# Queries in 576 columns instead of 640, and their positive part formed on GpSimd

## The chip, the cores and the metric

The kernel runs on one core of a Trainium2 chip. The metric is the device time of one execution in microseconds (us), given as the median of several runs. A profile of one execution stands beside it. Engines are called as the profile calls them: PE is TensorE, PEld its weight load, DVE is VectorE, ACT is ScalarE, POOL is GpSimd, and SP is SyncE, which here issues the transfers.

## The reference

An attention with a linear memory beside it is followed by two feed-forward products. B is 4, H is 8, S is 576, D is 64; the two products have 2048 and 1536 inner columns on a width of 512 and 2304 tokens.

```python
scores = q @ k^T / sqrt(D), causal;  a = softmax(scores);  local = a @ v
phi(x) = where(x > 0, x, exp(x) - 1) + 1            # = min(exp(x), 1) + max(x, 0)
mem_out = (phi(q) @ M_prev) / (phi(q) @ z_prev + 1e-6)
out = g * mem_out + (1 - g) * local                  # g = sigmoid(beta), one per head
x = out as [B*S, H*D];  h = x @ w_in
g2 = softplus(h);  x2 = g2 @ w_out
y = ((x2 @ w_a) * (x2 @ w_b)) @ w_2
```

## The kernel before

Sixteen attention units come first, one for each batch and pair of heads; a head lies in 64 of the 128 partitions. Each unit loads q and k turned (`qr`, `kr`), splits them into a rounded part and a rest (`qh`, `ql`, `kh`, `kl`), forms three products of these parts for the scores (L517), and takes mask, minimum and scale of the scores on DVE (L527, one instruction each for four blocks of each of two heads). ACT takes the exponentials (L531), PE turns them (L597, L614), ACT and DVE copy them out of the PSUM banks (L603, L605, L617), and PE multiplies them with v (L627, L647). The last 64 queries of two units go through L669 and L538 together.

The memory path of a unit is `prep_v` (L496 to L499: ACT forms exp(q) in `ph` and max(q, 0) in `pos`), `prep_v2` (L502: DVE forms `ph = min(ph, 1) + pos`), and `memory` (L545: PE multiplies `ph` with the memory in L555; DVE forms `nm` in L559 and L560 and `mo` in L561). `memory` of unit n uses PSUM banks 2 and 3, between the scores of unit n+1 and the turns of unit n. `pos` is one buffer, `ph` has two. Behind it the sums of the exponentials (`ss` on POOL, L582, and `rs` on DVE, L587) are turned (L570), copied (`rt`, L571), sent to a small DRAM tensor `rsd` and read back to all partitions as `rb` (L573, L576); `xx = po * rb` (L643, L655) ends the unit, and SP stores it (L660).

From the first units on, DVE and POOL also prepare the first feed-forward stage: L758, L759, L761 and L762 on DVE rebuild pieces of `w_in` from `raw`; L771 and L343 on POOL form their sums and rests; L801 reads finished tokens back from `xs` into `raw`. After the attention, PE runs the products of the first stage (L876) and later stages (L876, L1020) to the end.

The program is recorded as steps. `Plan.order` orders all steps of all engines once, at build time, in a simulated run with estimated durations; steps with the longest chain behind them go first, and PE takes attention before the first stage. Two rules in it concern POOL: DVE steps that read and write only SBUF are not placed while a POOL step runs, and a POOL step waits for the last such DVE step placed before it. Each engine then executes its own list in order.

In the kernel before, q has 640 columns. Columns 512 to 639 hold the last 64 queries of the two heads of a pair, each in 64 columns of its own with zeros in the other head's. L669 reads `u.qr[r, 512 + 64 * j : 576 + 64 * j]` and L555 reads column blocks of 64 from `ph`.

Of the kernel before, what the change touches and what calls it, by code (L numbers as in the profile page):

```python
# [12 lines left out]
AF = mybir.ActivationFunctionType  # L13
ALU = mybir.AluOpType
PSUM = bass.MemoryType.PSUM

B, H, S, D = 4, 8, 576, 64
NP = H // 2
# [305 lines left out]
def tile_kernel(ctx: ExitStack, tc: tile.TileContext, qt, kt, vt, mz, be, w_in, w_out, w_a, w_b, w_2, out):  # L324
    nc = tc.nc
    plan = Plan(tc)
    V, A, G, PE, SP = (
        Engine(plan, n, e) for n, e in (("DVE", nc.vector), ("ACT", nc.scalar), ("POOL", nc.gpsimd), ("PE", nc.tensor), ("SP", nc.sync))
    )

    def f(ap):
        return ap.bitcast(F32)

    def rnd(eng, o, i):
        if eng is A:
            A.activation(out=o, in_=i, func=AF.Copy)  # L336
        elif eng is V:
            V.tensor_copy(out=o, in_=i)
        else:
            G.tensor_scalar(out=o, in0=i, scalar1=1.0, scalar2=0.0, op0=ALU.mult, op1=ALU.add)  # L340

    def sub(eng, o, a, b):
        eng.tensor_tensor(out=o, in0=a, in1=b, op=ALU.subtract)  # L343
# [7 lines left out]
    bank = plan.track(nc.alloc_psum_tensor("bank", [128, 8, 512], F32).ap())  # L351
# [12 lines left out]
    def put(name, words, *at, dtype=F32):  # L364

        tag = name + "_" * (name in where)
        where[name] = [plan.buffer(f"{tag}{i}", words, a, dtype) for i, a in enumerate(at)], [0]

    def take(name):
        bufs, turn = where[name]  # L370
        turn[0] += 1
        return bufs[(turn[0] - 1) % len(bufs)]

    def space(lo):

        at = [lo]

        def next_(words):
            at[0] += (words + 7) & ~7
            return at[0] - ((words + 7) & ~7)  # L380

        next_.at = at
        return next_
# [12 lines left out]
    put("raw", 2048, RAW, RAW + 2048)  # L396
    early, late, spare = space(X1), space(X2), space(SUMS)
    more = space(WL + 7168)
    for n, words in (("kr", S), ("qr", 640), ("qh", 512), ("ql", 512), ("kh", S), ("kl", S), ("ph", 640)):
        at = [early(words), early(words)] + [more(words)] * (n in ("kr", "qr"))  # L400
        put(n, words, *at, dtype=F32R if n[1] in "hl" and n != "ph" else F32)
    put("pos", 640, early(640))
    w3 = [early(512) for _ in range(3)]
    put("eTrue", 512, *w3, spare(512), *(late(512) for _ in range(4)))
    put("eFalse", 256, *(spare(256) for _ in range(4)), *(late(256) for _ in range(4)))
# [26 lines left out]
    for j in range(2):  # L432
        G.affine_select(
            out=mask2[64 * j : 64 * j + 64, 1, 224:], in_=mask2[64 * j : 64 * j + 64, 1, 224:], compare_op=ALU.is_ge, fill=MASKED,
# [3 lines left out]
    both = (top, low)  # L438
# [24 lines left out]
    class Unit:  # L463
# [7 lines left out]
        def loads_k(self):  # L471
            b, p = self.b, self.p
            self.kr, self.qr = take("kr"), take("qr")
            first = b == p == 0
            for c, d in ((0, 256), (256, 640)) if first else ((0, 640),):
                SP.dma_start(out=self.kr[:, c : min(d, S)], in_=kt[b, p][:, c : min(d, S)])
                (A if first else SP).dma_start(out=self.qr[:, c:d], in_=qt[b, p][:, c:d])

        def loads_v(self):
# [5 lines left out]
        def prep_k(self, first=False):  # L485
            kr, qr = self.kr, self.qr
            self.qh, self.ql, self.kh, self.kl = (take(n) for n in ("qh", "ql", "kh", "kl"))
            e = V if first else G
            for c, d in ((0, 256), (256, 640)) if first else ((0, 640),):
                k, q = slice(c, min(d, S)), slice(c, min(d, 512))  # L490
                rnd(e, self.kh[:, k], kr[:, k])
                A.activation(out=self.qh[:, q], in_=qr[:, q], func=AF.Copy)
                sub(e, self.kl[:, k], kr[:, k], f(self.kh[:, k]))
                sub(e, self.ql[:, q], qr[:, q], f(self.qh[:, q]))

        def prep_v(self):  # L496
            self.ph, self.pos = take("ph"), take("pos")
            A.activation(out=self.ph, in_=self.qr, func=AF.Exp)
            A.activation(out=self.pos, in_=self.qr, func=AF.Relu)  # L499

        def prep_v2(self):
            V.scalar_tensor_tensor(out=self.ph, in0=self.ph, scalar=1.0, in1=self.pos, op0=ALU.min, op1=ALU.add)  # L502
# [42 lines left out]
        def memory(self, k):  # L545
            p, ph, mz = self.p, self.ph, mzs[self.b % 2]
            self.mo = mo = blocks(take("mo"))
            nm = take("nm")
            banks = bank[:, k : k + 2]
            s = banks[:, :, 0:325].rearrange("p j (c e) -> p j c e", c=5)  # L550
            for c in range(5):
                for half in both:
                    at = slice(128 * c + half.start, 128 * c + half.stop)
                    for j, r in self.rows:
                        PE.matmul(  # L555
                            out=s[half, j, c], lhsT=ph[r, at], rhs=mz[r, p], start=c == 0, stop=True, skip_group_check=True,
                        )
            by = lambda t: t.rearrange("p (j c) -> p j c", j=2)
            V.scalar_tensor_tensor(out=by(nm), in0=s[:, :, :, 64], scalar=1e-6, in1=by(self.rs), op0=ALU.add, op1=ALU.mult)  # L559
            V.reciprocal(out=nm, in_=nm)  # L560
            V.tensor_tensor(  # L561
                out=mo.rearrange("p c (j e) -> p j c e", j=2), in0=s[:, :, :, 0:64],
                in1=by(nm).unsqueeze(3).to_broadcast([128, 2, 5, 64]), op=ALU.mult,
            )
# [98 lines left out]
    def tails(at):  # L663

        for x in range(2):
            for u, k in at:
                for j, r in u.rows:
                    c = x ^ j
                    PE.matmul(  # L669
                        out=bank[both[j], k + c, :288], lhsT=u.qr[r, 512 + 64 * j : 576 + 64 * j], rhs=u.kr[r, 288 * c : 288 * c + 288],  # L670
                        start=True, stop=True, skip_group_check=True,
                    )
        for u, k in at:
            u.score_tail(k)
# [3 lines left out]
    def attention():  # L678
# [16 lines left out]
        for n in range(nu + 2):  # L695
# [24 lines left out]
            if cur:  # L720
                if n % 2 == 0:
                    nxt.begin()
                    tails(((cur, 0), (nxt, TAIL)))
                cur.sums()
                cur.over()
# [517 lines left out]
```

## Time and profile before

| what | value |
|---|---|
| median of 3 runs | 922.59 us (921.78 to 922.73) |
| profiled execution | 922.7 us, of which the profiled span is 920.9 us |
| granted TensorE clock | 1.0 over the whole span |
| busy PE, DVE, ACT, POOL | 907.3, 790.7, 565.3, 99.6 us |
| moved by DMA | 172.16 MB |

A share of busy time is a mean over very different stages. The attention ends near 176 us; POOL works only up to 169 us. Matmuls are pipelined, so PE counts as busy also where one matmul waits a little behind another.

### The profile page before, as it was taken

The numbers are of one execution on the slowest core, as the hardware profiler recorded it, in microseconds if no ns is written. First come the engines' busy times: TensorE is split into PE (matmuls) and PEld (weight loads), VectorE is DVE, ScalarE is ACT, GpSimd is POOL, SyncE is SP. The second block draws the span as 40 slices with busy tenths as digits, with TensorE's granted clock in tenths as the row PEclk, the third lists the DMA queues.
The fourth block names the chain that finished last, engine by engine and source line by source line (L and its number), as shares of the span: only waits on it lengthen the run. The fifth ranks groups of instructions, "written<-read, shape, count | busy, mean of one in ns | idle before, by whom it ended". The sixth has DMA issues, their size and how long they took to land.

```text
span 920.9 us, 17618 instructions
## 1 busy us (share of the span) xinstructions
PE 907.3 (99%) x6556; PEld 868.8 (94%) x6556; DVE 790.7 (86%) x1503; ACT 565.3 (61%) x1124; POOL 99.6 (11%) x140
## 2 busy tenths in 40 slices
PE   6999999999999999999999999999999999999998
PEld 4777777899999999999999999999999999999998
DVE  6999999889999758988599999988899666998683
ACT  7999999677666675744456655444444344555443
POOL 6445686100000000000000000000000000000000
PEclk9999999999999999999999999999999999999999
DMA  7656553368899889572620445455657156672701
GB/s 233 189 156 180 183 165 114 112 238 265 301 303 304 296 292 384 207 250 81 231 85 7 177 149 180 146 167 179 217 181 234 45 183 184 234 243 91 217 26 52
DMA packets 84838, 172.16 MB, mean 187 GB/s; under 512 B 8320, under 2 KB 60944, under 8 KB 82064
## 3 DMA queue, kind: packets, MB, share of 16 engines
q1 hardware_dynamic: 84320, 170.70, 56.4%
q8 instruction: 51, 0.84, 0.4%
q10 hardware_dynamic: 432, 0.33, 0.1%
q14 instruction: 35, 0.29, 0.1%
HBM read 110.90 MB, written 60.10 MB: 186 GB/s over the span
## 4 chain that ended last, share of the span: by engine, by line
PE 95%; DVE 2%; DMA 1%; issue 0%; SPq 0%; ACT 0%; DVEq 0%
PE bank L876 47%; PE bank L1020 33%; PE bank L627 4%; PE bank L597 3%; PE bank L517 3%; PE bank L555 1%; PE bank L669 1%; PE bank L647 1%; DVE eTrue L527 1%; PE bank L614 1%; DMA rb<-rsd 1%; PE bank L635 1%; DMA kr<-kt 0%; DVE ph L502 0%; DVE eT L538 0%
## 5 line engine op out<-in xcount | busy, mean ns | idle before, releaser
L346 DVE TENSOR_TENSOR s<-bank,s 128x384 f32<-128x384 f32 x216 | 118.0, 554 | 39.6 <-PE bank L876 30.5
L854 ACT ACTIVATE s<-bank 128x384 f32<-128x384 f32 x72 | 35.0, 486 | 80.7 <-PE bank L876 51.5
L343 DVE TENSOR_TENSOR t<-t,t 128x1536 f32<-128x1536 f32 (+1 forms) x48 | 74.6, 1554 | 0.4
L876 PE MATMUL bank<-x1h,w 128*128 128x384 f32 x240 | 70.7, 335 | 0.0
L876 PE MATMUL bank<-x5h,w 128*128 128x384 f32 x240 | 70.7, 335 | 0.0
L876 PE MATMUL bank<-x7h,w 128*128 128x384 f32 x240 | 70.6, 334 | 0.0
L876 PE MATMUL bank<-x3h,w 128*128 128x384 f32 x240 | 70.5, 334 | 0.0
L876 PE MATMUL bank<-x6h,w 128*128 128x384 f32 x240 | 70.5, 334 | 0.0
L876 PE MATMUL bank<-x4h,w 128*128 128x384 f32 x240 | 70.5, 334 | 0.0
L876 PE MATMUL bank<-x2h,w 128*128 128x384 f32 x240 | 70.5, 334 | 0.0
L336 ACT ACTIVATE w<-wf 128x256 fp32r<-128x256 f32 (+1 forms) x100 | 50.1, 501 | 19.6 <-DVE w L343 15.1
L912 ACT ACTIVATE s<-s 128x384 f32<-128x384 f32 x72 | 37.5, 523 | 33.2 <-DVE s L346 32.8
L851 ACT ACTIVATE s<-bank 128x384 f32<-128x384 f32 x72 | 34.9, 485 | 32.2 <-PE bank L876 14.9
L336 ACT ACTIVATE gx1h<-t 128x768 fp32r<-128x768 f32 x37 | 31.4, 848 | 34.0 <-PE bank L1020 33.5
L336 ACT ACTIVATE gx2h<-t 128x768 fp32r<-128x768 f32 x37 | 31.4, 847 | 34.0 <-PE bank L1020 32.9
L343 DVE TENSOR_TENSOR w<-wf,w 128x256 fp32r<-128x256 f32 (+1 forms) x90 | 47.5, 528 | 3.9 <-ACT w L336 3.5
L336 ACT ACTIVATE gx0h<-t 128x768 fp32r<-128x768 f32 x37 | 31.3, 846 | 30.6 <-PE bank L1020 29.1
L760 ACT ACTIVATE raw<-raw 128x512 f32<-128x512 f32 (+1 forms) x54 | 43.2, 801 | 9.8 <-DVE raw L759 9.2
L343 DVE TENSOR_TENSOR gx1l<-t,gx1h 128x768 fp32r<-128x768 f32 x37 | 35.4, 956 | 13.5 <-ACT gx1h L336 13.3
L343 DVE TENSOR_TENSOR gx0l<-t,gx0h 128x768 fp32r<-128x768 f32 x37 | 35.4, 957 | 13.0 <-ACT gx0h L336 12.8
L857 ACT ACTIVATE s<-bank 128x384 f32<-128x384 f32 x72 | 35.2, 489 | 16.2 <-PE bank L876 12.1
L336 ACT ACTIVATE gx3h<-t 128x768 fp32r<-128x768 f32 x36 | 30.4, 845 | 23.8 <-PE bank L1020 23.7
(340 smaller groups left out, 2992.1 us busy)
## 6 DMA issues: line engine op xcount, KB each, us to landing
gs<-s SPq DMA_DIRECT2D x96, 192.0 KB
t<-gs SPq DMA_DIRECT2D x24, 768.0 KB
us<-s SPq DMA_DIRECT2D x72, 192.0 KB
t<-us SPq DMA_DIRECT2D x12, 768.0 KB
raw<-w_out SPq DMA_DIRECT2D x8, 1024.0 KB
raw<-w_in SPq DMA_DIRECT2D x12, 512.0 KB
raw<-w_a SPq DMA_DIRECT2D x12, 512.0 KB
raw<-w_b SPq DMA_DIRECT2D x12, 512.0 KB
```

The lines of the kernel that those rows point to most:

```text
L336: A.activation(out=o, in_=i, func=AF.Copy)
L343: eng.tensor_tensor(out=o, in0=a, in1=b, op=ALU.subtract)
L346: eng.tensor_tensor(out=o, in0=a, in1=b, op=ALU.add)
L517: PE.matmul(out=s[:, j, at : at + L], lhsT=a[r, qc], rhs=b[r, 0:L], start=t == 0, stop=t == 2, skip_group_check=True,)
L627: PE.matmul(out=self.po[both[j], 128 * k :], lhsT=self.vr[:, k, 64 * j : 64 * j + 64], rhs=a, start=False, stop=k == 3, skip_group_check=True,
L760: A.activation(out=f(high), in_=f(high), func=AF.Identity, scale=REBIAS)
L851: A.activation(out=self.s1, in_=bank["b"], func=AF.Copy)
L854: A.activation(out=self.s5, in_=bank["c"], func=AF.Copy)
L857: A.activation(out=self.s2, in_=bank["b"], func=AF.Copy)
L876: PE.matmul(out=o, lhsT=w(n, a, k), rhs=x[n][c][:, k], start=start and k == t == 0, stop=k == 1 and t == 2, skip_group_check=True,)
L912: A.activation(out=s, in_=s if bank is None else bank, func=AF.Softplus)
L1020: PE.matmul(out=o, lhsT=self.w[n][a][:, u, 128 * m : 128 * m + 128], rhs=x[c][:, j], start=start and u == t == 0, stop=u == self.nu - 1 an ...
```

## The change

q is laid out in 576 columns: both heads' last 64 queries stand in columns 512 to 575, each in its own 64 partitions. The buffers of q, `ph` and `pos` shrink from 640 to 576 words, so the exponential on ACT and L502 on DVE work on 576 columns. max(q, 0) is formed by POOL instead of ACT. L555 reads columns 512 to 575 for both halves of the last block. The host no longer fills zeros.

```diff
-    for n, words in (("kr", S), ("qr", 640), ..., ("kl", S), ("ph", 640)):
+    for n, words in (("kr", S), ("qr", S), ..., ("kl", S), ("ph", S)):
...
-    put("pos", 640, early(640))
+    put("pos", S, early(S))
...
         def prep_v(self):
             self.ph, self.pos = take("ph"), take("pos")
             A.activation(out=self.ph, in_=self.qr, func=AF.Exp)
-            A.activation(out=self.pos, in_=self.qr, func=AF.Relu)
+            G.tensor_scalar(out=self.pos, in0=self.qr, scalar1=0.0, scalar2=0.0, op0=ALU.max, op1=ALU.add)
...
-                    at = slice(128 * c + half.start, 128 * c + half.stop)
+                    at = slice(128 * c + half.start, 128 * c + half.stop) if c < 4 else slice(512, S)
...
-                        out=bank[both[j], k + c, :288], lhsT=u.qr[r, 512 + 64 * j : 576 + 64 * j], rhs=u.kr[r, 288 * c : 288 * c + 288],
+                        out=bank[both[j], k + c, :288], lhsT=u.qr[r, 512:S], rhs=u.kr[r, 288 * c : 288 * c + 288],
...
-    qt = np.zeros((B, NP, 128, 640), q.dtype)
...
+        "qt": arr(split(q).transpose(0, 1, 2, 4, 3).reshape(B, NP, 128, S)),
```

Since the durations of steps change, `Plan.order` gives other lists for DVE, ACT, POOL and SP. PE's list stays, but for one place at the end of the attention, where four matmuls of L876 move from ahead of L615 of unit 15 to behind its L653.

The first place is DVE's list at the start of the program, where unit 0 (`ph0_78`, `nm0_129`, `mo0_103`) and the scores of unit 1 (`eTrue4_85` to `eFalse5_94`) meet. Before:

```order
L443 RECIPROCAL gt0_59<-gt0_59 128x8
L502 SCALAR_TENSOR_TENSOR ph0_78<-ph0_78,pos0_80 128x640
L538 ISA eT0_97,mn0_127<-bank,mask20_57 128x576
...
L527 ISA eFalse4_93,mn1_128<-bank,mask10_56 128x128
...
L559 SCALAR_TENSOR_TENSOR nm0_129<-bank,rs0_133 128x10
L527 ISA eTrue7_88,mn1_128<-bank,mask10_56 128x512
...
L560 RECIPROCAL nm0_129<-nm0_129 128x10
L571 COPY rt0_107<-bank 9x128
L561 TENSOR_TENSOR mo0_103<-bank,nm0_129 128x2x5x64
L527 ISA eFalse7_96,mn1_128<-bank,mask10_56 128x256
```

And of the change, at the same place:

```order
L443 RECIPROCAL gt0_59<-gt0_59 128x8
L538 ISA eT0_97,mn0_127<-bank,mask20_57 128x576
...
L527 ISA eTrue7_88,mn1_128<-bank,mask10_56 128x512
...
L527 ISA eFalse7_96,mn1_128<-bank,mask10_56 128x256
...
L527 ISA eFalse5_94,mn1_128<-bank,mask10_56 128x128
...
L502 SCALAR_TENSOR_TENSOR ph0_78<-ph0_78,pos0_80 128x576
L559 SCALAR_TENSOR_TENSOR nm0_129<-bank,rs0_133 128x10
L560 RECIPROCAL nm0_129<-nm0_129 128x10
L571 COPY rt0_107<-bank 9x128
L561 TENSOR_TENSOR mo0_103<-bank,nm0_129 128x2x5x64
```

L502 of unit 0 moved from ahead of the first L538 to behind all scores of unit 1, and `nm`, `rt` and `mo` moved behind it.

The second place is PE's list there, which is the same in both programs; L555 reads `ph0_78`, L570 turns the sums, L597 turns the exponentials:

```order
L517 MATMUL bank<-kh1_75,ql1_73 128x512 x2
L555 MATMUL bank<-mz0_105,ph0_78 64x65 x20
L570 MATMUL bank<-ident0_55,rs0_133 10x128
L597 MATMUL bank<-ident0_55,eFalse0_89 128x128
L597 MATMUL bank<-ident0_55,eFalse2_91 128x128
```

Nothing moved here: L555 of unit 0 stands ahead of all turns of unit 0, and of everything that follows.

The third place is SP's list around units 10 and 11, where `rb0_121` and `rb1_122` bring back the sums of both. Before:

```order
L660 DMA xs1<-xx1_124 128x384
L660 DMA xs2<-xx1_124 128x192
L483 DMA vr0_100<-vt 64x128
L801 DMA raw1_63<-xs0 128x1536
L573 DMA rsd11<-rt1_108 9x128
L576 DMA rb0_121<-rsd10 64x576 x2
L576 DMA rb1_122<-rsd11 64x576 x2
```

And of the change:

```order
L573 DMA rsd10<-rt0_107 9x128
L660 DMA xs1<-xx1_124 128x384
L660 DMA xs2<-xx1_124 128x192
L573 DMA rsd11<-rt1_108 9x128
L576 DMA rb0_121<-rsd10 64x576 x2
L576 DMA rb1_122<-rsd11 64x576 x2
```

L801, a read of 768 KB, no longer stands just ahead of these small transfers; it comes 20 transfers later, after the units 12 and 13 were sent.

## Rows read from the trace of the kernel before

**Rows 1.** The page's fourth part: the chain that ended last, shares by engine.

```profile
PE 95%; DVE 2%; DMA 1%; issue 0%; SPq 0%; ACT 0%; DVEq 0%
```

**Rows 2.** Windows: length; busy of PE, PEld, DVE, ACT, POOL; clock, DMA, GB/s.

```profile
24.40:44.80 20.40, 20.36 (x286) 15.72 (x286) 20.24 (x67) 19.91 (x54) 8.97 (x12) 1.00 0.61 189
44.80:65.20 20.40, 20.25 (x284) 15.72 (x284) 20.24 (x67) 18.48 (x52) 9.00 (x13) 1.00 0.52 159
65.20:85.50 20.30, 20.15 (x284) 15.71 (x284) 20.11 (x67) 18.95 (x54) 10.92 (x16) 1.00 0.50 151
85.50:105.50 20.00, 19.98 (x282) 15.53 (x282) 19.79 (x66) 19.94 (x57) 10.07 (x14) 1.00 0.68 199
105.50:125.20 19.70, 19.70 (x285) 15.39 (x284) 18.89 (x64) 18.70 (x53) 16.20 (x19) 1.00 0.56 174
125.20:146.10 20.90, 19.99 (x290) 15.49 (x288) 18.85 (x63) 20.47 (x58) 17.35 (x19) 1.00 0.47 138
...
176.00:921.00 745.00, 741.58 (x4276) 740.83 (x4275) 627.48 (x981) 404.63 (x687) 0.00 (x0) 1.00 0.57 191
```

**Rows 3.** Timeline of DVE, 10 to 27 us: start, duration, instruction, idle before it.

```profile
11.11 0.77 DVE L502 SCALAR_TENSOR_TENSOR ph<-ph,pos 128x640 f32<-128x640 f32 x1
12.35 0.76 DVE L538 CUSTOM_DVE_ANT_0 eT<-bank,mask 128x576 f32<-128x576 f32 x1 [0.47 <-PE bank L669]
...
16.79 0.21 DVE L560 RECIPROCAL nm<-nm 128x10 f32<-128x10 f32 x1
...
17.06 0.80 DVE L561 TENSOR_TENSOR mo<-bank,nm 128x640 f32<-128x640 f32 x1
17.79 0.40 DVE L527 CUSTOM_DVE_ANT_0 eFalse<-bank,mask 128x256 f32<-128x256 f32 x1
...
18.34 1.46 DVE L605 TENSOR_SCALAR aT<-bank,og 128x512 f32<-128x512 f32 x2
```

**Rows 4.** Timeline of PE, 14 to 25 us.

```profile
14.75 0.86 PE L555 MATMUL bank<-mz,ph 64*64 64x65 f32 x40
16.24 0.28 PE L570 MATMUL bank<-ident,rs 128*10 128x128 f32 x1 [0.63 <-DVE mn L527]
...
17.91 0.33 PE L597 MATMUL bank<-ident,eFalse 128*128 128x128 f32 x1 [0.27 <-DVE mo L561]
...
20.99 0.28 PE L570 MATMUL bank<-ident,rs 128*10 128x128 f32 x1 [0.56 <-DVE rs L587]
...
23.25 0.50 PE L517 MATMUL bank<-kh,qh 64*128 64x512 f32 x2 [0.57 <-ACT aT L603]
...
24.38 0.81 PE L555 MATMUL bank<-mz,ph 64*64 64x65 f32 x40 [0.17 <-DVE ph L502]
```

**Rows 5.** Groups by line and shape, DVE, 24.4 to 105.5 us: busy, mean ns, idle.

```profile
L527 DVE CUSTOM_DVE_ANT_0 eTrue<-bank,mask 128x512 f32<-128x512 f32 x16 | 10.7, 682 | 0.0
L527 DVE CUSTOM_DVE_ANT_0 eTrue<-bank,mask 128x384 f32<-128x384 f32 x16 | 8.2, 545 | 0.0
L502 DVE SCALAR_TENSOR_TENSOR ph<-ph,pos 128x640 f32<-128x640 f32 x9 | 7.4, 826 | 0.0
...
L759 DVE SCALAR_TENSOR_TENSOR raw<-raw 128x512 uint32<-128x512 uint32 x4 | 2.7, 670 | 0.0
...
L761 DVE TENSOR_SCALAR raw<-raw 128x512 f32<-128x512 f32 x4 | 1.6, 411 | 0.0
```

**Rows 6.** Groups by line and shape, all engines, 20 to 165 us.

```profile
L499 ACT ACTIVATE pos<-qr 128x640 f32<-128x640 f32 x15 | 11.0, 735 | 3.0 <-DVE ph L502 2.9
...
L340 POOL TENSOR_SCALAR kh<-kr 128x576 fp32r<-128x576 f32 x12 | 8.2, 680 | 6.9 <-PE bank L517 5.7 <-DMA kr<-kt 1.1
```

**Rows 7.** The chain in order of time, one piece: start, length, what.

```profile
124.55 5.73 DMA rb<-rsd
```

**Rows 8.** Timeline of all engines, 26.3 to 29 us.

```profile
26.47 1.41 POOL L343 TENSOR_TENSOR kl<-kr,kh 128x576 fp32r<-128x576 f32 x1
...
27.64 0.93 DVE L502 SCALAR_TENSOR_TENSOR ph<-ph,pos 128x640 f32<-128x640 f32 x1
```

More of the change, by code (lines that the diff above doesn't have):

```diff
@@ L398, in tile_kernel @@
     more = space(WL + 7168)
-    for n, words in (("kr", S), ("qr", 640), ("qh", 512), ("ql", 512), ("kh", S), ("kl", S), ("ph", 640)):
+    for n, words in (("kr", S), ("qr", S), ("qh", 512), ("ql", 512), ("kh", S), ("kl", S), ("ph", S)):
         at = [early(words), early(words)] + [more(words)] * (n in ("kr", "qr"))
         put(n, words, *at, dtype=F32R if n[1] in "hl" and n != "ph" else F32)
-    put("pos", 640, early(640))
+    put("pos", S, early(S))
     w3 = [early(512) for _ in range(3)]
@@ L474, in loads_k @@
             first = b == p == 0
-            for c, d in ((0, 256), (256, 640)) if first else ((0, 640),):
-                SP.dma_start(out=self.kr[:, c : min(d, S)], in_=kt[b, p][:, c : min(d, S)])
+            for c, d in ((0, 256), (256, S)) if first else ((0, S),):
+                SP.dma_start(out=self.kr[:, c:d], in_=kt[b, p][:, c:d])
                 (A if first else SP).dma_start(out=self.qr[:, c:d], in_=qt[b, p][:, c:d])
@@ L488, in prep_k @@
             e = V if first else G
-            for c, d in ((0, 256), (256, 640)) if first else ((0, 640),):
-                k, q = slice(c, min(d, S)), slice(c, min(d, 512))
+            for c, d in ((0, 256), (256, S)) if first else ((0, S),):
+                k, q = slice(c, d), slice(c, min(d, 512))
                 rnd(e, self.kh[:, k], kr[:, k])
@@ L1195 @@
     swap = lambda w: arr(w.reshape(-1, 128, 2, 2, 256)[:, :, :, ::-1]).reshape(w.shape)
-    qt = np.zeros((B, NP, 128, 640), q.dtype)
-    turned = split(q).transpose(0, 1, 2, 4, 3)
-    qt[..., 0:512] = turned[..., 0:512].reshape(B, NP, 128, 512)
-    for p in range(NP):
-        for j in range(2):
-            h = 64 * (j ^ (p & 1))
-            qt[:, p, 64 * j : 64 * j + 64, 512 + h : 576 + h] = turned[:, p, j, :, 512:576]
     def by_unit(a, axis):
@@ L1211 @@
     arrays = {
-        "qt": qt,
+        "qt": arr(split(q).transpose(0, 1, 2, 4, 3).reshape(B, NP, 128, S)),
         "kt": arr(split(k).transpose(0, 1, 2, 4, 3).reshape(B, NP, 128, S)),
```

## The prediction

> **What bounds the kernel now.** I read the chain first: 95% of the span hangs on PE and 2% on DVE [rows 1]. From 176 us to the end PE is busy 741.6 of 745.0 us [rows 2], and PE's list there is unchanged. So nothing behind 176 us can be won, and the question is only when PE gets there. Before 176 us I read the windows, cut where L555 of every second unit starts, so that each holds two units. The same PE list takes 20.4, 20.4, 20.3, 20.0, 19.7 and 20.9 us [rows 2]. The fastest, 19.7 us, has PE busy for all of it and DVE with 0.8 us to spare; I take it as what PE needs for two units. In the first three DVE is busy 20.24, 20.24 and 20.11 us, all but 0.2 us: there DVE sets the pace, and PE loses 0.7, 0.7 and 0.6 us, then 0.3. The sixth loses 1.2 us; a piece of the chain there is a read of `rb` that took 5.73 us [rows 7], queued behind L801, a read of 768 KB. All these losses are 3.5 us. Ahead of 24.4 us PE waits in larger pieces [rows 4]. These two places are all that the change can touch.
>
> **Part by part.** *Work taken from ACT and DVE.* ACT loses 16 of L499, 0.735 us each by its record [rows 6], and 64 columns of 16 exponentials. ACT has 0.1 to 1.9 us free in every window and is not what PE waits for, so I price this at nothing; the cover is DVE's own work, and were ACT the pace, 1.5 us per two units would come back. For DVE a 64-column piece costs half of 0.682 - 0.545 us, 0.07 us [rows 5]. Records overlap the next instruction a little (`mo`: 0.80 us by record, 0.73 us to the next start [rows 3]), so L502 occupies 0.75 us now and 0.68 us after; L759 0.60 us; L761 0.34 us.
>
> *The start.* L502 of unit 0 ran at 11.11 us in front of a DVE wait of 0.47 us that it cost nothing to fill [rows 3]. Now it stands behind unit 1's scores, while L555, which reads its result, still stands ahead of all PE work of unit 0. In DVE's list `nm`, `rt` and `mo` go behind it. There L560, L571 and L561 took 16.79 to 17.79 us, 1.00 us; without them the scores end at 18.34 - 1.00 = 17.34 us. Add 0.68 for L502 and 0.1 us to the start on PE (L597 started 0.05 us after `mo` ended): L555 starts at 18.1 instead of 14.75 us. It takes 0.81 us, so L570 follows at 18.9 instead of 16.24 us [rows 3, 4]: PE is 2.7 us late. It wins back waits that stood on that way: 0.27 for `mo`, 0.56 for `rs`, 0.57 for ACT, 0.17 us for L502 of unit 1 [rows 4], which now runs earlier in the list and is no longer late. That leaves 1.15 us at 24.38 us; small waits below these may take 0.15 more. I take +1.0 us. Bounds: 0 if the score instructions, freed of `nm` and `mo`, run ahead of PE by more than I think, and 2.7 us if none of the waits is won back.
>
> *The stretch from 24.4 to 105.5 us, with DVE as the pace.* From the lists: in the first window DVE has one L502 more and one L759 less; in the second one L502 less (and L762 becomes L759); in the third one L762 more, one L758 and one L759 less; in the fourth one L502 and two L761 less, one L758 more. L762 and L758 are close to L759 and L761. With 0.07 us less in each L502 DVE needs 20.24 + 0.68 - 0.14 - 0.60 = 20.2; 20.24 - 0.75 - 0.14 = 19.4; 20.11 - 0.14 + 0.60 - 0.34 - 0.60 = 19.6; 19.79 - 0.75 - 0.07 + 0.34 - 0.68 = 18.6 us. Where that is under 19.7 us PE is the pace. The sum is 20.2 + 3 x 19.7 = 79.3 us, against 81.1 now: -1.8 us. In the third window L502 stands right ahead of the scores of a new unit, which L555 waits for; I give back 0.3 us: -1.5 us. Bounds: -2.3 us (PE alone, 4 x 19.7) and 0.
>
> *105.5 to 176 us.* The fifth window has room for one L502 more. In the sixth L801 is gone from ahead of `rb`, but the rebuilding of the last `w_in` pieces has come here: L759 and two L761 more. DVE needs 18.85 + 0.60 + 0.68 - 0.14 = 20.0 us, against 20.9 now: -0.9 us. The last two L762 run near 150 us, 1.2 us more against one L502 less, 0.75 us, in a stretch with little room: +0.3 us. Together -0.6 us, bounds -1.4 and +0.5 us.
>
> *POOL.* Its new instruction is not in the trace. The nearest is L340, of the same size and with one input: 0.68 us [rows 6]; the far bound is the two-input L343, 1.41 us [rows 8]. I take 0.68 us, 10.9 us for 16. POOL is busy 39 of 81.1 us between 24.4 and 105.5 us [rows 2], so it has room. But its work for the first units of the next stage (sums and rests of `w_in` and x) gets later: by the lists 22 instructions of it follow the last new one. POOL was busy 16.2 and 17.4 us in the two windows in which it did much of this work, against 9 to 11 us before [rows 2], so some 13 us of it move back behind 150 us, where POOL was idle for more than half of the time; it ends perhaps 8 us later than at 169 us, near 177. PE takes these parts one after the other during its first two units of the stage, behind 176 us. I count them as just in time, with some 2 us of cover. If that cover is gone, PE waits for what is missing, one for one.
>
> *One rule against the change.* When L502 met a POOL instruction with two inputs, it took 0.93 instead of 0.81 us: POOL had run from 26.47 to 27.88 us, and L502 started at 27.64 [rows 5, 8]. The Trainium skill, SBUF — State Buffer, section "SBUF: two separate sides", says that a DVE operation with two SBUF inputs and a POOL operation that reads SBUF lock the shared port pair against each other, and that the loser waits for the whole of the other. By that rule L502 would have done nothing before 27.88 us and lasted 0.24 us longer; the row shows 0.12. The sum by the rule would add 10.9 us of locked time against DVE's L502, L759 and L762; by the row it adds a tenth of a microsecond for each meeting. I take the row.
>
> *The rest.* The read of q shrinks by 32 of 320 KB per unit; no wait of PE or DVE in [rows 3, 4] is for it: nothing. The moved four matmuls of L876 give PE 0.7 us less to do before L615, but DVE ahead of it has no L343 any more: nothing.
>
> **Sum.** 922.7 us of the profiled execution + 1.0 - 1.5 - 0.6 = 921.6 us. That execution is 0.1 us above the median of the runs, so I forecast **921.5 us** against 922.59.
>
> **Rivals.** *PE is the pace throughout.* All losses after 24.4 us go, 3.5 us, and the start costs 0.6: 919.7 us. For it speaks that DVE loses 80.4 - 77.8 = 2.6 us of work up to 105.5 us; against it, the first window, where hardly any of it goes.
>
> *The start costs all, little comes back.* +2.0 us at the start, -1.5 for the rest: 923.1 us. For it speaks the order of PE's list, which makes every matmul wait for `ph0_78`; against it, the 1.57 us of waits that lie behind it.
>
> *POOL and DVE block each other: slower.* Place: DVE's L502, L759 and L762, 24 instructions with two inputs from SBUF, between 24 and 165 us. POOL's share between 24.4 and 105.5 us rises from 48% to (39 + 8 x 0.68) / 81.1 = 55%, so 13 of them meet POOL if nothing keeps them apart. At 0.1 us a meeting it is nothing beside DVE's room. At half of an L343, 0.7 us, it is 9 us. From 0.25 us a meeting, 3.2 us in all on the path, the kernel is slower: 924.7 us. That the other eight L502 of [rows 5] took 0.81 us in the mean, (9 x 0.826 - 0.93) / 8, speaks against it: POOL's waits kept them apart; for it, that POOL has less time left to wait. The skill's section above is the rule that would bring this about.
>
> *The change does nothing at the end.* If start and stretch cancel, it is 922.6 us; this is inside my forecast's own range.
>
> **Chances and range.** My forecast, from -2.2 to 0 us, 44%; PE as the pace 28%; a dear start 13%; blocking 15%. A difference under 0.2%, 1.8 us, can hardly be told from none with this kernel. Faster by more (under 920.75): all of the PE case and a small part of mine, 34%. Slower by more: 14%. The rest, 52%, is the same. The range 919.3 to 924.0 us leaves out part of the PE case and most of blocking. The likeliest case alone spans 920.4 to 922.6.
>
> **What would show it.** Right: L555 of unit 0 starts near 18 us, and of unit 1 near 25.4 instead of 24.38; the next windows take 20.2, 19.7 to 20.0, and 19.7 us; no `rb` wait of DVE near 130 us; POOL ends near 177 us and PE has no gap from 170 to 190 us. Wrong: L502 of unit 0 starts at another time than 17.3; L502 records of 1 us and more with POOL beside them; DVE idle in a window that still takes over 20 us, which would name ACT or POOL as the pace; PE gaps after 176 us that wait for w or x rests from POOL.

## The result: slower by 0.7%, and the profile after

The changed kernel takes 929.81 us (median of 4 runs, 929.14 to 930.3) where the kernel before took 922.66 us beside it: 1.007 times as long, 95% interval 1.0058 to 1.0082. The forecast was 921.5 us with 924.0 us as its upper end. The profiled execution took 929.68 us, with a span of 927.9 us.

The chain that ended last, by engine, was 95% PE and 2% DVE [rows 1]. After the change:

```profile
PE 87%; DVE 5%; POOL 3%; issue 2%; DMA 1%; ACT 0%; SPq 0%; DVEq 0%; POOLq 0%; ACTq 0%
```

POOL, which had no share in it, now has 3%. What it has to do is in the groups by line and shape, 20 to 165 us, which answer to [rows 6]:

```profile
L499 POOL TENSOR_SCALAR pos<-qr 128x576 f32<-128x576 f32 x15 | 32.0, 2135 | 5.3 <-DVE ph L502 3.7 <-DMA rb<-rsd 1.0
...
L340 POOL TENSOR_SCALAR kh<-kr 128x576 fp32r<-128x576 f32 x13 | 8.9, 682 | 2.0 <-PE bank L517 1.7
```

The two lines have the same engine, kind of instruction and size, and one takes 2.135 us, the other 0.682 us. They also differ in the type that they write, float32 against fp32r; the run with the short L499 below writes float32 too and settles that.

Windows, cut as in [rows 2] (length; busy of PE, PEld, DVE, ACT, POOL; clock, DMA, GB/s), with one more from 97 to 132 us:

```profile
24.40:44.80 20.40, 20.13 (x282) 15.30 (x281) 19.96 (x66) 16.49 (x49) 14.46 (x15) 1.00 0.54 164
44.80:65.20 20.40, 19.87 (x284) 15.27 (x283) 20.00 (x67) 17.47 (x50) 13.65 (x14) 1.00 0.50 153
65.20:85.50 20.30, 20.30 (x291) 16.04 (x290) 19.92 (x66) 16.99 (x50) 12.87 (x14) 1.00 0.47 152
85.50:105.50 20.00, 19.40 (x280) 14.91 (x279) 19.35 (x64) 17.78 (x53) 16.44 (x18) 1.00 0.65 191
105.50:125.20 19.70, 18.98 (x278) 14.53 (x277) 17.64 (x58) 18.19 (x54) 17.04 (x19) 1.00 0.47 141
125.20:146.10 20.90, 18.98 (x257) 13.87 (x257) 19.30 (x65) 15.40 (x45) 13.77 (x13) 1.00 0.38 114
...
97.00:132.00 35.00, 32.49 (x449) 25.19 (x447) 30.88 (x99) 28.83 (x84) 29.58 (x30) 1.00 0.43 136
```

The last window in the kernel before:

```profile
97.00:132.00 35.00, 34.18 (x483) 26.08 (x479) 33.04 (x111) 33.88 (x96) 27.32 (x30) 1.00 0.50 156
```

Up to 125.2 us DVE has a little more idle time than before, as forecast, but PE loses 0.7 and 1.9 us in the two windows from 105.5 us on (0 and 0.9 before), and neither DVE nor ACT fills them. In the 35 us from 97 us PE is idle for 2.5 us, against 0.8 before.

The starts of L555 on PE, one mark per unit, show where the time goes (us from the start of the span; the last three columns are of experiments below):

| unit | before | changed | short L499 | unit 0 on ACT | q + 1 |
|---|---|---|---|---|---|
| 0 | 14.75 | 19.16 | 18.93 | 15.73 | 16.88 |
| 1 | 24.38 | 27.55 | 26.16 | 24.96 | 25.59 |
| 8 | 95.87 | 99.61 | 97.31 | 97.10 | 97.06 |
| 9 | 105.52 | 109.91 | 106.73 | 108.22 | 106.75 |
| 10 | 115.88 | 120.27 | 117.09 | 119.68 | 117.10 |
| 11 | 125.22 | 132.27 | 126.75 | 130.74 | 127.11 |
| 15 | 163.88 | 170.51 | 165.08 | 169.53 | 165.12 |

The changed kernel is 3.2 us late at unit 1, 3.7 at unit 8, 7.1 at unit 11, 6.6 at unit 15: two losses, one at the start and one between units 8 and 11. The first on PE's and DVE's timelines (answering to [rows 4] and [rows 3]):

```profile
19.16 1.36 PE L555 MATMUL bank<-mz,ph 64*64 64x65 f32 x40 [3.30 <-issue]
```

```profile
12.11 0.76 DVE L538 CUSTOM_DVE_ANT_0 eT<-bank,mask 128x576 f32<-128x576 f32 x1 [1.16 <-PE bank L669]
...
15.89 0.69 DVE L527 CUSTOM_DVE_ANT_0 eTrue<-bank,mask 128x512 f32<-128x512 f32 x1 [1.38 <-PE bank L517]
...
18.30 0.76 DVE L502 SCALAR_TENSOR_TENSOR ph<-ph,pos 128x576 f32<-128x576 f32 x1
```

L502 of unit 0 stands where the list put it, behind unit 1's scores, and PE stands still for 3.3 us until it is done. The page puts that wait down to "issue"; that it is for L502 is read from the list and from L502's end at 19.06 us.

The second loss on the chain in order of time (start, length, what), 122 to 131 us:

```profile
120.86 1.28 POOL w L343
122.15 0.66 POOL kh L340
122.80 0.07 issue
122.88 1.42 POOL kl L343
124.29 0.66 issue
...
125.00 2.13 POOL pos L499
...
127.21 0.22 POOL ss L582
...
127.45 0.04 DVE rs L587
...
127.58 0.69 DVE aT L605
128.27 1.10 DVE ph L502
129.38 0.66 DVE aT L605
130.04 0.60 DVE aT L617
```

From 120.86 to 127.43 us the links are work of POOL, one instruction behind the other, L499 the longest; the sums `ss` stand behind it, and DVE's `rs` waits for them. The 0.66 us at 124.29 us, which the chain calls "issue", is L499's wait for L502, which has still to read the one buffer of `pos`; L502 itself ran until `kl` had ended:

```profile
122.88 1.42 POOL L343 TENSOR_TENSOR kl<-kr,kh 128x576 fp32r<-128x576 f32 x1
123.27 1.64 DVE L502 SCALAR_TENSOR_TENSOR ph<-ph,pos 128x576 f32<-128x576 f32 x1
125.00 2.13 POOL L499 TENSOR_SCALAR pos<-qr 128x576 f32<-128x576 f32 x1 [0.70 <-DVE ph L502]
```

In the run called "q + 1" below, this stretch of the chain, 118 to 131 us, holds PE and 0.04 us of "issue".

### The profile page after: what moved, and what is told of

Read it like the earlier page. It is cut to its first block, busy times and chain, and to the rows that moved or that the text cites. A ratio compares the mean times of both kernels' runs of the same rounds, so it can differ in the third digit from the quotient of the medians.

```text
span 927.9 us, 17660 instructions
## 1 busy us (share of the span) xinstructions
PE 910.1 (98%) x6556; PEld 871.0 (94%) x6556; DVE 792.4 (85%) x1503; ACT 555.9 (60%) x1108; POOL 134.3 (14%) x156
## 4 chain that ended last, share of the span: by engine, by line
PE 87%; DVE 5%; POOL 3%; issue 2%; DMA 1%; ACT 0%; SPq 0%; DVEq 0%; POOLq 0%; ACTq 0%
PE bank L876 47%; PE bank L1020 33%; PE bank L627 2%; PE bank L597 2%; PE bank L517 1%; DVE eTrue L527 1%; POOL pos L499 1%; PE bank L555 1%; DVE aT L605 1%; DVE ph L502 1%; DMA xs<-xx 1%; DMA kr<-kt 1%; PE bank L647 0%; DVE eT L538 0%; DVE eFalse L527 0%
## 5 line engine op out<-in xcount | busy, mean ns | idle before, releaser
L343 DVE TENSOR_TENSOR t<-t,t 128x1536 f32<-128x1536 f32 (+1 forms) x48 | 74.5, 1552 | 0.4
L876 PE MATMUL bank<-x1h,w 128*128 128x384 f32 x240 | 70.6, 334 | 0.0
L876 PE MATMUL bank<-x5h,w 128*128 128x384 f32 x240 | 70.5, 334 | 0.0
L876 PE MATMUL bank<-x6h,w 128*128 128x384 f32 x240 | 70.5, 334 | 0.0
L876 PE MATMUL bank<-x2h,w 128*128 128x384 f32 x240 | 70.5, 334 | 0.0
L876 PE MATMUL bank<-x3h,w 128*128 128x384 f32 x240 | 70.5, 334 | 0.0
L876 PE MATMUL bank<-x7h,w 128*128 128x384 f32 x240 | 70.5, 334 | 0.0
L876 PE MATMUL bank<-x4h,w 128*128 128x384 f32 x240 | 70.5, 334 | 0.0
L531 ACT ACTIVATE eTrue<-eTrue,mn 128x512 f32<-128x512 f32 (+1 forms) x64 | 42.0, 658 | 18.1 <-DVE mn L527 16.4
L343 DVE TENSOR_TENSOR w<-wf,w 128x256 fp32r<-128x256 f32 (+1 forms) x90 | 47.2, 525 | 3.3 <-ACT w L336 2.7
L343 DVE TENSOR_TENSOR gx1l<-t,gx1h 128x768 fp32r<-128x768 f32 x37 | 35.3, 954 | 12.5 <-ACT gx1h L336 12.1
L343 DVE TENSOR_TENSOR gx0l<-t,gx0h 128x768 fp32r<-128x768 f32 x37 | 35.3, 954 | 12.1 <-ACT gx0h L336 11.7
```

The costliest lines, as they stand in the source:

```text
L531: A.activation(out=e, in_=e, func=AF.Exp, scale=-1.0, bias=mn[:, n : n + 1], accum_out=sm[:, n : n + 1])
L876: PE.matmul(out=o, lhsT=w(n, a, k), rhs=x[n][c][:, k], start=start and k == t == 0, stop=k == 1 and t == 2, skip_group_check=True,)
```

## The experiments

Diffs are against the changed kernel, unless said otherwise. All ratios are to the kernel before, beside it on the same chip, with their 95% intervals; 0.1% is 0.92 us.

### 576 columns alone, 640 columns with POOL

```diff
-            G.tensor_scalar(out=self.pos, in0=self.qr, scalar1=0.0, scalar2=0.0, op0=ALU.max, op1=ALU.add)
+            A.activation(out=self.pos, in_=self.qr, func=AF.Relu)
```

> q in 576 columns, and its positive part on ACT as before: one part of the change alone. In DVE's and POOL's lists unit 0's L502 stands ahead of L538 again, as before the change. Duration theory (POOL's L499 takes 2.13 us where 0.68 was priced, and what stands behind it on POOL comes late): none of it is left, so L555 of unit 0 starts near 14.7 us and the time is 921.9 us, the kernel before less 0.07 us for each L502. Order theory (the list in which unit 0's L502 stands behind unit 1's scores costs the start, whatever L499 lasts): the same, 921.9 us. Rival: the narrower q itself does harm (other places of buffers, PE's last chunk of 64 columns): 925 us or more.

Measured: 922.75 us, 0.9993 (0.9984 to 1.0002). The narrower q does no harm and gains nothing that can be told from zero.

The second run is the kernel before with its L499 written as the minus line above.

> q in 640 columns as before, and its positive part on POOL: the other part alone. Here unit 0's L502 stands ahead of L538 in DVE's list. Duration theory: L499 takes 640/576 of 2.13 us, about 2.35 us, and POOL's sums, kl and ql behind it are late: 929 us or more. Order theory: with L502 at its old place the start costs little, L555 of unit 0 under 16.5 us, and the time is 925 us or less. Lock theory (L502 waits for POOL's kl and ql whole): L502 records of over 1 us wherever one of these stands beside it, time by their number, 0.4 us each.

Measured: 931.51 us, 1.0088 (1.0075 to 1.0102); L499 took 2.346 us in the mean of 16. So POOL's part alone makes the kernel slower, as the duration theory had it. The order theory said 925 us or less and missed, but its own condition was not met: L502 of unit 0 did run early, at 11.01 us, and still L555 of unit 0 started at 18.55 us and not under 16.5, since POOL formed `mz` (L456), which L555 reads too, only behind its second L499:

```profile
18.55 0.81 PE L555 MATMUL bank<-mz,ph 64*64 64x65 f32 x40 [1.34 <-POOL mz L456]
```

So this run doesn't weigh the order against the duration; the run with unit 0 on ACT, below, does.

### The same lists with a short L499

```diff
-            ... scalar1=0.0, scalar2=0.0, op0=ALU.max, op1=ALU.add)
+            ... scalar1=1.0, scalar2=0.0, op0=ALU.mult, op1=ALU.add)
```

> The changed kernel with L499 as q times 1 plus 0 (it leaves out the maximum, so the positive part isn't formed): the operations of L340, and the same order of every engine, instruction by instruction. L499 should last 0.68 us. Duration theory: about 922 us, what the forecast had for this price. Order theory: the start stays late, L555 of unit 0 near 19 us, and only the loss of 2.7 us between 120 and 132 us goes: 927 us. Lock theory: L502 still meets kl and ql: 929 us.

Measured: 926.2 us, 1.0026 (1.0016 to 1.0035); L499 took 0.674 us. With no instruction in another place, 0.44%, 4.1 us, are gone: that much is duration alone. The lock theory's 929 us missed. PE's loss between 97 and 132 us is gone too:

```profile
97.00:132.00 35.00, 35.00 (x522) 26.55 (x519) 33.06 (x114) 31.94 (x95) 25.56 (x30) 1.00 0.43 133
```

But 0.26% stay, and L555 of unit 0 stays at 18.93 us, as the order theory said. The duration has the larger part of it; whether the rest is the start's order is open (see "What stays open"). The single times are of two kinds, 924.0 to 924.5 us (three) and 925.9 to 927.0 us (seven); the profile is of the first kind.

### Which operation is slow

```diff
+            forms = (
+                dict(scalar1=0.0, scalar2=0.0, op0=ALU.max, op1=ALU.add),
+                dict(scalar1=0.0, scalar2=None, op0=ALU.max),
+                dict(scalar1=0.0, scalar2=0.0, op0=ALU.add, op1=ALU.max),
+                dict(scalar1=0.0, scalar2=1.0, op0=ALU.max, op1=ALU.mult),
+            )
+            G.tensor_scalar(out=self.pos, in0=self.qr, **forms[order.index(self) % 4])
```

> The changed kernel with L499 in four forms in turn, four units each, all of which form the positive part: max then add 0, max alone, add 0 then max, max then times 1. Duration theory, if the maximum is what POOL is slow at: all four near 2.1 us, and the time that of the changed kernel, 929 to 930 us. If the pair of operations is what is slow: max alone near 0.7 us and the others 2.1 us, time near 928 us.

Measured: one time of 931.54 us. POOL's timeline, 9 to 40 us, has the four forms in turn (L499 is L505 here):

```profile
9.68 2.13 POOL L505 TENSOR_SCALAR pos<-qr 128x576 f32<-128x576 f32 x1
19.58 1.66 POOL L505 TENSOR_SCALAR pos<-qr 128x576 f32<-128x576 f32 x1
25.66 2.14 POOL L505 TENSOR_SCALAR pos<-qr 128x576 f32<-128x576 f32 x1
32.61 2.15 POOL L505 TENSOR_SCALAR pos<-qr 128x576 f32<-128x576 f32 x1 [1.99 <-DMA rb<-rsd]
```

The maximum alone costs 1.66 us, and each of the second operations tried 0.48 us more; the order of the two makes no difference. The pair mult and add, of L340, is the one that costs 0.68 us. It is the operation, then, and the first theory holds in its milder form: dropping the second would have saved nearly a quarter of L499.

### The start, and the same lists once more

Unit 0's L499 goes back to ACT, the other 15 stay on POOL:

```diff
+            A.activation(out=self.pos, in_=self.qr, func=AF.Relu) if self is order[0] else G.tensor_scalar(...)
```

> The changed kernel with L499 of unit 0 alone on ACT; the other 15 stay on POOL at 2.13 us. L502 of unit 0 stands ahead of L538 again. Theory in three parts (order at the start 1.5 us, clock after PE's wait there 2.2 us, duration of L499 3.4 us): L555 of unit 0 starts under 16 us, the granted clock stays 1.00 to 24.4 us, and the time is 3.4 us above the kernel before. Rival, that duration alone counts and the start is won back: 6 us above or more.

Measured: 929.74 us, 1.0065 (1.0051 to 1.0079). L555 of unit 0 starts at 15.73 and of unit 1 at 24.96 us, so the start is mended, and nothing comes of it: between units 8 and 11 the loss is now larger (table). The rival holds: with the long L499 a better start is lost again, and the order of the start falls as the main cause.

The next run has this kernel's lists, instruction by instruction, and the positive part in another form:

```diff
+            A.activation(... AF.Relu) if self is order[0] else G.tensor_scalar(... scalar1=1.0, scalar2=1.0, op0=ALU.mult, op1=ALU.add)
-            V.scalar_tensor_tensor(out=self.ph, in0=self.ph, scalar=1.0, in1=self.pos, op0=ALU.min, op1=ALU.add)
+            V.scalar_tensor_tensor(... op0=ALU.min, op1=ALU.add if self is order[0] else ALU.max)
```

> q in 576 columns, unit 0's positive part on ACT, and for the other 15 units L499 on POOL as q times 1 plus 1, with max in place of add as the second operation of L502: the larger of q + 1 and min(exp(q), 1) is the same function. L499 should last 0.68 us. Theory in three parts: nothing of them is left, and the time is that of 576 columns alone, 0.5 us under the kernel before, within 1 us. Rival, that POOL's work itself (waits for L502, locked ports) costs: 2 us above the kernel before or more.

Measured: 923.39 us, 0.9997 (0.9988 to 1.0006); L499 took 0.673 us. Against the run before, 1.0065 - 0.9997 = 0.68%, 6.3 us, hang on the 15 times 1.46 us of L499 alone; L502 with max takes the same 0.75 us where POOL is not beside it. The windows from 97 to 132 us of the two (first the long L499, then the short):

```profile
97.00:132.00 35.00, 32.31 (x465) 24.37 (x465) 32.08 (x102) 29.76 (x86) 27.83 (x28) 1.00 0.40 129
```

```profile
97.00:132.00 35.00, 34.96 (x518) 26.45 (x516) 34.02 (x115) 32.87 (x98) 24.67 (x29) 1.00 0.45 144
```

PE goes from 2.7 us of idle time to none. The work of POOL itself, waits and meetings with DVE included, is not what costs, as long as it is short.

### The clock at the start

In the changed kernel's profile the granted clock is 0.68 in the mean from 19 to 24.4 us, behind PE's wait of 3.3 us, so partly at the lower level of 1.2 GHz. (It was 0.58 and 0.56 in the two stretches of 2 us from 12 us on, ahead of that wait, too; and in the run with the short L499 it was 1.00 behind a wait of 3.31 us.) To keep PE busy there:

```diff
+            [PE.transpose(out=bank[:, 6, 0:128], in_=ident, identity=ident) for _ in range(16 * (self is order[0]))]
```

> The changed kernel with 16 transposes of the identity (128x128, about 0.16 us each, results not used) on PE right ahead of L555 of unit 0, where PE waits 3.3 us; nothing else in any engine's list differs. Clock theory: PE is busy in the wait, the granted clock stays 1.00 between 19 and 24.4 us where the changed kernel had 0.50 to 0.71, and the time falls by 2.2 us, to 4.9 us above the kernel before. Rival, that DVE and POOL set the pace there and PE's clock is covered: no change, 7 us above.

Measured: 931.43 us, 1.0083 (1.0068 to 1.0099). The two kernels from 19 to 24.4 us, the changed one first:

```profile
19.00:24.40 5.40, 5.25 (x67) 5.15 (x68) 3.06 (x8) 5.19 (x16) 4.60 (x5) 0.68 0.62 209
```

```profile
19.00:24.40 5.40, 4.67 (x72) 4.13 (x72) 3.79 (x8) 5.40 (x17) 4.59 (x5) 1.00 0.83 280
```

The transposes took 1.97 us of PE's wait, and 1.40 us of it remained. The clock stayed at 1.00, and PE then waited 1.00 us more at 25.62 us, for DVE's `aT`; L555 of unit 1 started at 27.80 against 27.55 us. The clock theory falls: the slower clock there is covered. The same transposes in the run with the short L499:

> The run with the short L499 (q times 1 plus 0, which leaves out the maximum) with the 16 transposes on PE ahead of L555 of unit 0. That run had times of two kinds, near 924.2 us and near 926.4 us. Theory that the clock after PE's wait of 3.3 us makes the two kinds: all times near 924.2 us, the ratio to the kernel before near 1.001. Rival, that they have another cause, as the changed kernel, which gained nothing from the transposes, lets expect: both kinds again, ratio 1.0026 or more.

Measured: 925.36 us, 1.002 (1.001 to 1.003), single times from 922.94 to 926.07 us, with a mean granted clock of 0.998 to 1.00 in each. In the run without the transposes the clock had gone with the two kinds: 0.998 to 1.00 in the three lower times, 0.996 in six of the seven higher ones. Times up to 926.07 us come without that dip too, so the clock alone doesn't make the spread; what else does stays open.

These two runs with transposes are a third pair whose lists are the same and whose L499 differs: 1.0083 - 1.002 = 0.63%, 5.8 us, with no dip of the clock on record at the start in either profile.

### A list made for the real price

```diff
-            s.time = n * 2.1 + 210 if two else n * 0.82 + 200
+            s.time = n * 2.1 + 210 if two else n * (3.35 if kw.get("op0") == ALU.max else 0.82) + 200
```

> The changed kernel with the measured 2.13 us for L499 in the planner's prices (3.35 ns a column instead of 0.82), so that the order of DVE, ACT, POOL and SP is made for the real duration; PE's list is the same. Theory that the loss is a list made for a wrong price: most of the 3.4 us by which the changed kernel stands over the run with the short L499 comes back, 3.5 us above the kernel before or less. Rival, that 16 times 1.46 us more on POOL can't be planned away: 6 us above the kernel before or more, as with 640 columns, where L502 of unit 0 stood early too.

Measured: 926.79 us, 1.0037 (1.0023 to 1.0051). With L499 still at 2.13 us, 0.33%, 3.0 us, come back: some of the duration's cost came from a list that planned 0.67 us. The profile shows where. PE's loss between 97 and 132 us is gone, though POOL is busier there than in the changed kernel:

```profile
97.00:132.00 35.00, 34.91 (x506) 27.52 (x506) 33.65 (x109) 31.54 (x91) 30.46 (x33) 1.00 0.53 161
```

From L555 of unit 8 (101.12 us) to that of unit 11 (130.49) it takes 29.4 us, as in the kernel before; the changed kernel takes 32.7. So by this profile the second loss comes of the long L499 in a list made for a short one, and not of POOL's work as such. What this list still loses lies at the start: PE waits 3.86 us in one piece ahead of 25.69 us, for DVE's `rs`, and L555 of unit 1 starts at 29.81 us.

### POOL's waits taken out of the ring

Two buffers for `pos`, and in the next run the planner's rule of waiting for DVE kept from POOL's small instructions:

```diff
-    put("pos", S, early(S))
+    put("pos", S, early(S), more(S))
```

```diff
-        s.port = s.eng == "POOL" or s.eng == "DVE" and ...
+        s.port = s.eng == "POOL" and n > 64 or s.eng == "DVE" and ...
```

> The changed kernel with two buffers for the positive part, so that POOL's L499 of a unit needn't wait until DVE's L502 of the unit before has read the one; L499 stays at 2.13 us, and the lists of all engines come out somewhat different. Theory that the loss is a ring, L502, then L499, then the sums and ql behind it, then DVE's next steps and L502 again: with one of its waits gone (3.7 us of POOL before L499) 2 to 3 us come back, 4 to 5 us above the kernel before. Rival, that POOL's busy time alone is what counts between 97 and 132 us: 6.5 us above or more.

Measured: 933.31 us, 1.0111 (1.0097 to 1.0124).

> The changed kernel with the planner's rule that a POOL instruction waits for DVE's last two-input SBUF instruction ahead of it taken off POOL's small ones (64 columns and fewer, the sums of L582 above all, which waited 11.9 us for L502). L499 stays at 2.13 us. L502 of unit 0 comes to stand ahead of L538. Theory of the ring: the sums no longer wait for L502, DVE's L587 gets them earlier, 2 to 3 us come back, 4 to 5 us above the kernel before. Rival, POOL's busy time alone: 6 us above or more.

Measured: 931.08 us, 1.0084 (1.0066 to 1.0102).

> The run with q + 1 on POOL and max in L502 (0.68 us each, unit 0 on ACT), with the planner's rule taken off POOL's small instructions. Theory of the ring: its waits for L502 shrink (POOL's L582 ahead of all), 0.5 to 1.5 us under the kernel before. Rival, PE is the pace there and has next to nothing to gain: within 0.5 us of the kernel before, as without this.

This is the second edit on the run with q + 1. Measured: 923.62 us, 1.0004 (0.9995 to 1.0013).

The ring theory, as I put it, missed all three times. The first edit hardly touched the wait it was meant for: L499 waited 3.7 us in all for L502 in the changed kernel and 3.4 us with two buffers. The second did: the sums' waits for L502 went from 11.9 us to none, and in the third run from 9.4 us to none, and no time came back. So nothing shows that the sums' waits cost; L499's were not taken out. With two buffers the stretch from unit 8 to unit 11 takes 29.8 us in the profile, hardly more than before, but that list loses 8.6 us ahead of it. All three runs have other lists than the runs they stand against, so they don't show how much a wait alone is worth.

### Which of the 16 cost

L499 on POOL for units 1 to 9 alone, then for units 10 to 15 alone, the rest on ACT:

```diff
+            A.activation(... AF.Relu) if order.index(self) not in range(1, 10) else G.tensor_scalar(... op0=ALU.max, op1=ALU.add)
```

> The changed kernel with L499 on POOL (2.13 us) for units 1 to 9 alone, before POOL has work of the next stage; units 0 and 10 to 15 on ACT. Theory of the crowded stretch (only beside POOL's work for the next stage, from 97 us on, does the longer L499 reach PE): at most 1 us above the kernel before. Rival, each of the 15 in the run with unit 0 on ACT costs alike, 6 us in all: 9/15 of it, 3.6 us above.

Measured: 924.52 us, 1.0009 (1.0 to 1.0018).

```diff
+            A.activation(... AF.Relu) if order.index(self) < 10 else G.tensor_scalar(... op0=ALU.max, op1=ALU.add)
```

> The changed kernel with L499 on POOL (2.13 us) for units 10 to 15 alone, the others on ACT. Theory of the crowded stretch: PE loses 2 us or more between 97 and 132 us, and the time is 4 us or more above the kernel before. Rival, each costs alike: 6/15 of 6 us, 2.4 us above.

Measured: 926.94 us, 1.0034 (1.0022 to 1.0045). Against 576 columns alone (0.9993), nine early ones cost 0.16%, 1.5 us, and six late ones 0.41%, 3.8 us: 0.16 and 0.63 us each. The windows from 97 to 132 us, early first, then late:

```profile
97.00:132.00 35.00, 34.99 (x527) 26.99 (x527) 34.32 (x116) 34.03 (x100) 21.25 (x25) 1.00 0.50 155
```

```profile
97.00:132.00 35.00, 33.19 (x465) 25.18 (x465) 31.39 (x104) 30.20 (x88) 29.53 (x30) 1.00 0.41 121
```

With the late ones POOL is busy 29.5 of 35 us, as in the changed kernel, and PE loses 1.8 us; with the early ones no L499 of POOL lies in this window, POOL has 21.3 us to do and PE loses nothing. With lists made for a short L499 the crowded stretch is where most of it is lost, though 3.1 us above the kernel before lies between the theory's 4 us and the rival's 2.4. The lists of these runs differ from one another, so the shares are rough.

## Why the prediction was wrong

**The step that failed is the price of POOL's new instruction.** "The nearest is L340, of the same size and with one input: 0.68 us [rows 6]; the far bound is the two-input L343, 1.41 us [rows 8]. I take 0.68 us, 10.9 us for 16." It took 2.135 us, 34.2 us for 16 (16 x 2.135). Size, kind and number of inputs were the same as L340's; the operation was not, and it decides. The far bound was too low as well. With the short L499 and the same lists the kernel came to 1.0026 times the kernel before, and the time falls by 4.1, 5.8 and 6.3 us in the three pairs of runs with the same lists that differ in this duration. This is shown. By which way the longer L499 reaches PE is shown in part: by POOL's late sums on the chain, and by a list that was made for 0.67 us.

The Trainium skill, GPSIMD Engine Reference, section "4.1 Engine selection", says of elementwise add, multiply and maximum that POOL is about two times slower with two inputs and that one input goes at roughly line rate. No run here measures that line rate, but one rate for all three does not hold: mult and add together take 0.68 us for 576 columns, the maximum alone 1.66 us, and the measurement decides.

**"So it has room" held only up to 97 us, with these lists.** There the nine early ones cost 0.16 us each. Behind it POOL forms the sums, `kl` and `ql` of the last units and the rests of the next stage, and its work became the chain. With the list made for 2.13 us there was room there too (PE idle for 0.1 of 35 us). The forecast looked at POOL's share of the time up to 105.5 us, and carried the later work only to the hand-over at 176 us. That hand-over was right in its result: POOL ended at 186.9 instead of 177 us, and PE had no gap from 160 to 200 us.

**The start was sized nearly right, and with the long L499 less was won back.** L502 of unit 0 was expected at 17.34 us and L555 at 18.1; the changed kernel had 18.30 and 19.16 us. About 1 us of that is PE's pace ahead of it (below): in the run with 576 columns alone, with the old place of L502, L555 started at 15.77 instead of 14.75 us. Against that run, the short L499 is 26.16 - 25.33 = 0.8 us late at unit 1, where I had 1.0. The changed kernel is 27.55 - 25.33 = 2.2 us late there.

**The 1.5 and 0.6 us from a lighter DVE did not come.** L502 became cheaper by the size that I took (0.82 to 0.75 us where POOL was not beside it), but 576 columns alone, which have this gain, came to 0.9993. In its profile L555 of unit 15 follows that of unit 1 by 138.71 us, against 139.50 before, so 0.8 us at most were won there, and a start 0.95 us later took them up. No run here shows which wait took the place of the rest. The prediction's windows were also not all cut where L555 starts: units 3, 5 and 7 start at 44.47, 64.74 and 85.04 us. The four stretches are 20.1, 20.3, 20.3 and 20.5 us and not 20.4, 20.4, 20.3 and 20.0; their sum, and with it the forecast's -1.8 us, is the same.

**The price of a meeting was too low, and the rival's part is not settled.** In the changed kernel L502 of unit 1 started at 23.44 us beside a `kl` of POOL that ran to 24.04 us:

```profile
22.62 1.42 POOL L343 TENSOR_TENSOR kl<-kr,kh 128x576 fp32r<-128x576 f32 x1
23.44 1.21 DVE L502 SCALAR_TENSOR_TENSOR ph<-ph,pos 128x576 f32<-128x576 f32 x1
```

It ended 0.61 us after `kl`, which is nearly its whole work. So did the other five, 0.61 to 0.62 us after a `kl` or `ql`, the longest with 1.64 us (shown above) and 1.19 us. My 0.1 us a meeting, from [rows 5, 8], was too low: that L502 had met only the last 0.24 us of a `kl` and ended 0.69 us after it, which fits these rows, at 640 columns. The 0.12 us that I read there was what was left of that `kl`, less some 0.1 us, and not a price for a meeting. The Trainium skill, SBUF — State Buffer, section "SBUF: two separate sides", has the loser wait for the whole of the other instruction; these rows agree to within 0.14 us (0.61 us behind the end, where L502 alone takes 0.75 us). Over all 16 this adds (0.46 + 0.19 + 0.05 + 0.89 + 0.44 + 0.06) = 2.1 us to DVE against 0.75 us each; the run with the short L499 has meetings too (1.48 and 0.98 us), and the run with q + 1, which has some, is no slower than before. So meetings by themselves don't make the kernel slower. But with the long L499 there are more of them, and some stand on the chain: of its stretch from 122 to 131 us, 0.66 us (L499's wait for the L502 of 1.64 us) and 0.44 us (the L502 of 1.19 us). In the run with unit 0 on ACT L502, L759 and L762 took 3.9 us longer in all than at 0.75 and 0.68 us each, in the run with q + 1 0.5 us. How much of the 6.3 us between these two came by that way is not shown.

**What stays open.** The change with a short L499 keeps 0.26%, of which the run with q + 1, with L502 of unit 0 at its old place, is free; that the start's order is the cause fits, but the two lists differ in other places too. How the cost of the duration is shared between POOL's own time and a list made for another price is known only by one run (3.0 us back with the right price). No version here is faster than the kernel before.

## What to carry to other kernels

Price an instruction on a row with the same engine, shape and operation; where the operation differs, no neighbour is a bound, and the range must say so. When work moves to an engine that looks idle, lay its new work beside that engine's fullest stretch, not beside its mean, and see what waits in its list behind the new work. And where a planner orders the program by prices, a wrong price costs twice: the instruction is longer, and the list is made for another one.

## What the runs showed of the hardware

POOL's tensor_scalar on 128x576 float32 takes 0.67 to 0.68 us with mult and add, 1.66 us with max alone, 2.13 to 2.15 us with max and one more operation; 2.35 us on 640 columns, so 3.3 ns a column ((2.346 - 2.135) / 64).

An L502 of DVE (two inputs from SBUF, 576 columns, 0.75 us alone) that started while POOL ran a `kl` or `ql` ended 0.61 to 0.62 us after POOL's instruction, in all six meetings of the changed kernel, whether 0.2 or 1.0 us of that was left.

The 16 matmuls of L669 near 10.7 us took 1.50 us in five of the sixteen profiles (before and changed kernel among them) and 2.50 us in the other eleven, with the same instructions and the same wait of 1.6 to 2.1 us ahead of them. The kernel before, and 576 columns alone:

```profile
10.92 1.50 PE L669 MATMUL bank<-kr,qr 64*64 64x288 f32 x16 [1.61 <-DVE mn L527]
```

```profile
10.67 2.50 PE L669 MATMUL bank<-kr,qr 64*64 64x288 f32 x16 [1.61 <-DVE mn L527]
```

In the five the trace's first record of a granted clock, at 1.00, begins at 8.8 to 9.5 us, ahead of L669, in the eleven from 13.8 us on, behind it; where no clock is on record, the 1.00 of a row is no reading. In three of the five the granted clock was then 0.52 to 0.62 from 12 to 16 us. So a start that differs by 1 us between two profiles needn't come from the change; the profile of before had neither the long L669 nor the low clock behind it.
